# Ranking TensorE's inputs over weight conversions in the schedule of a fused attention and two-MLP kernel

## The chip, the cores and the metric

The kernel runs on one core of a Trainium2 chip. The metric is the device time of one launch in microseconds (us). Three runs of the kernel before gave 895.55, 897.68 and 898.25 us.

## The reference

An attention with random features on 4 batches, 8 heads, 576 positions and 64 channels, then two MLPs on its 2304 rows of 512 channels:

```python
q_p, k_p = phi(q * scale), phi(k * scale)      # phi: exp(x @ omega.T - sq - max) / sqrt(m), m = 128
kv = einsum('bhsm,bhsd->bhmd', k_p, v)
z = sum(k_p, axis=2)
x = einsum('bhsm,bhmd->bhsd', q_p, kv) / (einsum('bhsm,bhm->bhs', q_p, z)[..., None] + 1e-06)
x = softplus(x @ w_in) @ w_out                 # 512 -> 2048 -> 512
x = ((x @ w1) * (x @ w2)) @ w3 @ w_out2        # 512 -> 1024 -> 1024 -> 512
```

The weights of the MLPs are 64-bit floats (`view(np.int64)`), everything else is 32-bit.

## The kernel before, in words

Every product is made of three matmuls (`mm3`): each operand x is split into a rounded part hi and a rest lo = x - hi, and hi*hi, hi*lo and lo*hi are summed in PSUM. So TensorE (PE) needs two split operands for each product, and making these splits is the work of the other engines.

The program has six stages, one after the other on PE: the K features (until about 67 us), the Q features with the attention's output (until 157 us), **Up1** (the product with w_in, then softplus; until 345 us), **down1** (the product with w_out; from 348 to 610 us), **Up2** (the products with w1 and w2, multiplied; until 790 us) and **down2** (until 894 us).

- *Up1 and Up2* go by 24 "quads" each (class `Quad`): one block of weights by one block of 768 tokens, as seven products of 128x384 instead of eight. ScalarE (ACT) copies the first product to SBUF (`p6`, L479), VectorE (DVE) forms the sums u and c of products (`add`, L473), two of them on the way to further sums; ACT then applies softplus (L503) or DVE multiplies (L525), and SyncE (SP) stores the results to DRAM (gd or pd). The four PSUM banks of a quad come free when its sums have read them.
- *down1 and down2* (function `down`) go by groups of token chunks; for each of 16 (or 8) row blocks f a tile `dn` is loaded by SP four steps ahead (L569), split by ACT (`dhi`, L575) and DVE (`dlo`, L576) one step ahead (`parts(m + 1)`), and multiplied into four PSUM banks (`mult`). down1's first group holds chunks 0 and 1, and 8 banks; then come chunks 2, 3 and 4 alone. Behind the last f of a chunk its four banks are evicted to tiles `y`, even ones by DVE (L612), odd ones by ACT (L610), and SP stores them to `yd` at once (`store_y`, L723).
- *Weight conversions* (class `Job`) turn a 64-bit block into 32-bit hi and lo on the chip: a load (L119, on ACT's queue), a relu on ACT (L126), four operations on DVE (L129, L135, L142, L149), for Up1 and Up2 three sums of blocks on DVE (L156, L159, L162), the casts thi (L188) and hi (L175) on ACT, and the rests tlo (L192) and lo (L180) on GpSimd (POOL). These operations stand in a list that `step` empties at a rate beside the products. w_out, w1, w2, w3 and the last weight are converted during Up1 and down1; eight products of w3 and the last weight (`fold`) run inside down1.

Order: the framework's scheduler fixes for each engine one order of instructions, before the program runs, from the order in which they were written down and from when it takes each to be ready. Each engine then works strictly through its own list, and an instruction that waits holds up what stands behind it on that engine. The small pools matter for this: 14 buffers `M_` hold dn, dhi, dlo, y, p6 and the sums; 2 hold raw weights; 4 hold f and t of a conversion; 8 hold finished weights; PSUM has 8 banks.

Of the kernel before, what the change touches and what calls it, by code (L numbers as in the profile page):

```python
# [19 lines left out]
F32 = mybir.dt.float32  # L20
# [3 lines left out]
AF = mybir.ActivationFunctionType  # L24
ALU = mybir.AluOpType
# [30 lines left out]
FOLD_RATE = 7.0  # L56
FOLD_AT = [42 + 3 * j for j in range(8)]
KEEP = 4


@with_exitstack
def body(ctx: ExitStack, tc: tile.TileContext, q, k, k_rest, v, v_rest, om_t, w_in, w_out, w12, w3, wo, out):
    nc = tc.nc
# [9 lines left out]
    def ps():  # L73
        return ps_.tile([128, 512], F32, tag="ps", name="ps")

    def mt(n=512, dt=F32, name="m"):
        return M_.tile([128, n], dt, tag="m", name=name)
# [10 lines left out]
    def mm3(o, ahi, alo, bhi, blo, first, last, **kw):  # L88
        matmul(o, ahi, bhi, first, False, **kw)
        matmul(o, ahi, blo, False, False, **kw)  # L90
        matmul(o, alo, bhi, False, last, **kw)
# [3 lines left out]
    yd = dr.tile([128, KD, NT], F32, name="yd")  # L95
# [15 lines left out]
    class Job:  # L111
        def __init__(self, src, n, place, pool, sums=False):
            self.src, self.n, self.place, self.pool, self.sums, self.done = src, n, place, pool, sums, False
            self.slots = 4 if sums else 2
            self.kept = None

        def load(self):
            self.raw = L_.tile([128, self.n], I64, tag="l", name="raw")
            nc.scalar.dma_start(out=self.raw, in_=self.src)  # L119

        def words(self, i, dt):
            return self.raw.bitcast(dt).rearrange("p (n w) -> p n w", w=2)[:, :, i]
# [77 lines left out]
    def job_ops(jobs):  # L200
        ops = [jobs[0].load, jobs[0].relu] + [x.load for x in jobs[1:2]]
        late = []
        for i, x in enumerate(jobs):
            ops += [x.floor, x.bits_a] + late + [x.bits_b, x.bits_c]
            y = [] if x.kept else x.splits()
            late = [x.spill] if x.kept else []
            nxt = [jobs[i + 2].load] if i + 2 < len(jobs) else []
            at = next((n + 1 for n, z in enumerate(y) if isinstance(z, tuple)), len(y))
            ops += y[:at] + nxt + y[at:]
            if i + 1 < len(jobs):  # L210
                ops.append(jobs[i + 1].relu)
        return ops + late

    def reload_ops(jobs):
        ops = [x.reload for x in jobs[:1]]
        for x, y in zip(jobs, jobs[1:] + [None]):
            z = x.splits()
            ops += z[:4] + ([y.reload] if y else []) + z[4:]
        return ops
# [13 lines left out]
    def step(rate):  # L233
        due[0] += rate
        while due[0] > 0:
            if not pump_one():
                due[0] = min(due[0], 2.0)
                break
            due[0] -= 1
# [5 lines left out]
    def need(x):  # L245
        until(lambda: x.done)

    win = [Job(w_in[i], 1024, jt, "J", True) for i in range(NF // 2)]
# [159 lines left out]
    def operands(c, src, pool):  # L408
# [27 lines left out]
        a11, a21 = lambda: a[0][0], lambda: a[0][1]  # L436
        a12, a22 = lambda: a[1][0], lambda: a[1][1]
        ops = [load(0), load(1)]
        ops += parts("a11", a11)
        ops += [total("s1", a21, a22, ALU.add), total("s2", lambda: s["s1"], a11, ALU.subtract)]  # L440
# [8 lines left out]
    class Quad:  # L449
# [20 lines left out]

        def add(self, y, bank, name):
            z = mt(N, name=name)
            nc.vector.tensor_tensor(out=z, in0=bank, in1=y, op=ALU.add)  # L473
            return z

        def begin(self):
            p6 = mt(N, name="p6")
            b1 = self.product("t2", "s2")
            nc.scalar.copy(out=p6, in_=b1)  # L479
            self.b2 = self.product("t3", "s3")  # L480
            self.b3 = self.product("t1", "s1")
            self.b0 = self.product("b11", "a11")
            self.u2 = self.add(p6, self.b0, "u2")
            u3 = self.add(self.u2, self.b2, "u3")
            self.c22 = self.add(u3, self.b3, "c22")
# [10 lines left out]
    class Up1(Quad):  # L496
# [3 lines left out]

        def put(self, dst, src, f, t):
            t = self.t + t * N
            nc.scalar.activation(out=dst, in_=src, func=AF.Softplus)  # L503
            nc.sync.dma_start(out=gd[2 * self.i + f][:, t:t + N], in_=dst)

        def begin(self):
# [11 lines left out]
    class Up2(Quad):  # L518
# [3 lines left out]

        def put(self, x, y, t):
            t = self.t + t * N
            nc.vector.tensor_tensor(out=y, in0=x, in1=y, op=ALU.mult)  # L525
            nc.sync.dma_start(out=pd[self.j][:, t:t + N], in_=y)

        def finish(self):
# [31 lines left out]
    def down(src, nf, weight, store, groups, before=None, tail=1):  # L560

        seq = [(*chunks[c], f) for g in groups for f in range(nf) for c in g]
        got, split_, acc = {}, {}, {}

        def load(m):
            if m < len(seq):
                t0, n, f = seq[m]
                got[m] = mt(n, name="dn")
                nc.sync.dma_start(out=got[m], in_=src[f][:, t0:t0 + n])  # L569

        def parts(m):
            if m < len(seq):
                n = seq[m][1]
                hi, lo = mt(n, FR, "dhi"), mt(n, FR, "dlo")
                nc.scalar.copy(out=hi, in_=got[m])  # L575
                nc.vector.tensor_tensor(out=lo, in0=got.pop(m), in1=hi.bitcast(F32), op=ALU.subtract)  # L576
                split_[m] = hi, lo

        def mult(m, d):
            t0, n, f = seq[m]  # L580
            hi, lo = split_[m]
            mm3(acc[t0][d], *weight(f, d), hi, lo, f == 0, f == nf - 1)
            if f == nf - 1:
                store(d, t0, n, acc[t0][d])

        for m in range(AHEAD):
            load(m)
        parts(0)
        yield
        for m, (t0, n, f) in enumerate(seq):  # L590
            if f == 0:
                acc[t0] = [ps()[:, :n] for _ in range(KD)]
            load(m + AHEAD)
            parts(m + 1)
            if before:
                before(m, f)
            if m < len(seq) - tail:
                for d in range(KD):
                    mult(m, d)
                split_.pop(m)  # L600
            step(DOWN_RATE[m // NF] if before else 1.0)
        for d in range(KD):
            for m in range(len(seq) - tail, len(seq)):
                mult(m, d)
        yield

    def evict_down(d, src, n, name):
        o = mt(n, name=name)
        if d % 2:
            nc.scalar.copy(out=o, in_=src)  # L610
        else:
            nc.vector.tensor_copy(out=o, in_=src)  # L612
        return o


# [39 lines left out]
    ln = LQ + LN  # L655
    lx = ln + XSLACK
    xo = {}
    queue += job_ops(win[:2])
    for u in range(nq + lx + 2):
        if u >= LQ and u - LQ < nq:  # L660
# [33 lines left out]
    for s in range(NW):  # L694
        n = min(WB, NF * 512 - WB * s)
# [9 lines left out]
    wo_j.append(Job(wo[NJ - 1], 512, lambda name: spare[name == "lo"], None))  # L705
    w12_k = w12_j[KEEP:]
    w3_j = [Job(w3[j], 1024, jt, "J") for j in range(NJ)]

    def fold(j):
        need(w3_j[j])  # L710
        acc = ps()
        for i in range(NJ):
            a = 128 * i
            mm3(acc, w3_j[j].hi[:, a:a + 128], w3_j[j].lo[:, a:a + 128], wo_j[i].hi, wo_j[i].lo, i == 0, i == NJ - 1)
        o = mt(name="w34")
        nc.scalar.copy(out=o, in_=acc)
        nc.sync.dma_start(out=wd[j], in_=o)
        free["J"] += 2
        if j == NJ - 1:
            free["X1"] += 2 * (NJ - 1)  # L720

    def store_y(d, t0, n, src):
        nc.sync.dma_start(out=yd[:, d, t0:t0 + n], in_=evict_down(d, src, n, "y"))  # L723

    def before_1(m, f):
        if m in FOLD_AT:
            fold(FOLD_AT.index(m))
            step(FOLD_RATE)
        last = min(NW - 1, (4 * f + 3) // (WB // 128))
        need(wout[last])  # L730
        if m > NF * (len(DOWN) - 1) and f:
            for s in range((4 * f - 4) // (WB // 128), NW):
                if 6 * s + 5 < 4 * f and not wout[s] in given:
                    given.append(wout[s])
                    free[wout[s].pool] += 2

    given = []
    d1 = down(gd, NF, w_slot, store_y, [[0, 1], [2], [3], [4]], before_1)

    def after_1(c):  # L740
# [5 lines left out]
    ready.clear()  # L746
    for x, f in zip(w12_k, wf[KEEP:]):
        x.kept = f
    queue += job_ops(wo_j + w3_j[:4] + [x for p in zip(w12_k, w3_j[4:]) for x in p] + w12_j[:2])
    for c in range(2):  # L750
        xo[c], ops = operands(c, yd, f"X{c}")
        queue += ops
    next(d1)
    for x in wout:
        if x not in given:
            free[x.pool] += 2


    xo[2], ops = operands(2, yd, "X1")
    queue += ops + job_ops(w12_j[2:KEEP]) + reload_ops(w12_k)  # L760
    w34 = {}
# [24 lines left out]
    def store_out(d, t0, n, src):  # L786
        nc.sync.dma_start(out=out[128 * d:128 * d + 128, t0:t0 + n], in_=evict_down(d, src, n, "o"))
# [77 lines left out]
```

## Time and profile before

| what | value |
|---|---|
| three runs | 895.55, 897.68, 898.25 us (median 897.68) |
| the profiled execution | 895.84 us, of which the span of instructions is 894.1 us |
| busy in the span: PE, its weight loads, DVE, ACT, POOL | 96%, 86%, 67%, 42%, 20% |
| mean granted clock of PE | 0.989 of full speed |

Times in the trace are microseconds from the start of the span. A busy share is an average over six stages, so stretches are read apart. A name such as `dlo<-dn,dhi` is the tile written and the tiles read; in the lists of waits the waiting instruction stands to the left of `<-`, what released it to the right.

### The profile page before, as it was taken

What the parts mean: (1) busy time and instruction counts of PE and PEld (TensorE: products, weight loads), DVE (VectorE), ACT (ScalarE), POOL (GpSimd) and SP (SyncE); (2) the same over time, 40 slices, a digit from 0 to 9 for tenths busy, and PEclk for the clock granted to TensorE, in tenths of its full rate; (3) what the DMA queues carried; (4) which work ended last, traced back from release to release, by engine and by line L of the source; (5) the groups of instructions that cost most, each with busy time, mean ns of one, the idle gap of its engine ahead of it and who ended that gap; (6) DMA issues with size and microseconds to landing.
All of it is one profiled execution on the core that took longest, in us unless ns stands there. A gap on an engine that the chain in (4) does not pass through costs nothing.

```text
span 894.1 us, 14621 instructions
## 1 busy us (share of the span) xinstructions
PE 856.4 (96%) x5496; PEld 766.3 (86%) x5496; DVE 600.5 (67%) x932; ACT 379.8 (42%) x796; POOL 179.0 (20%) x110
## 2 busy tenths in 40 slices
PE   6999999999998998999889999999999999999998
PEld 5887888999998997888668887899999999988887
DVE  4795788998755578887957676258995665563322
ACT  5686889554444355444343342153411111132221
POOL 2453321022122242222221121100132222000000
PEclk9997999999999999999999999999999999999999
DMA  9511454555543447656586763154322221364432
GB/s 356 190 66 48 120 167 131 186 200 200 184 147 111 168 154 259 218 181 232 170 285 226 259 247 131 59 166 140 137 101 77 77 71 54 108 216 142 141 118 95
DMA packets 72535, 141.68 MB, mean 158 GB/s; under 512 B 7056, under 2 KB 39952, under 8 KB 69392
## 3 DMA queue, kind: packets, MB, share of 16 engines
q1 hardware_dynamic: 65696, 100.89, 33.6%
q10 hardware_dynamic: 6768, 39.85, 13.4%
q8 instruction: 43, 0.70, 0.3%
q14 instruction: 28, 0.23, 0.1%
HBM read 94.05 MB, written 46.66 MB: 157 GB/s over the span
## 4 chain that ended last, share of the span: by engine, by line
PE 65%; DVE 15%; DMA 9%; issue 5%; ACT 3%; POOL 1%; SPq 1%; ACTq 0%; DVEq 0%; POOLq 0%
PE ps L86 63%; DVE f L129 2%; DVE f L142 2%; DVE c L473 2%; DVE f L149 2%; DMA dn<-gd 2%; DMA xq<-xd 2%; PE ps L367 1%; DVE f L135 1%; DMA raw<-in_w 1%; DVE s L422 1%; DMA xq<-yd 1%; DVE dlo L576 1%; DVE u L473 1%; PE ps L397 1%
## 5 line engine op out<-in xcount | busy, mean ns | idle before, releaser
L180 POOL TENSOR_TENSOR lo<-f,hi 128x512 fp32r<-128x512 f32 (+3 forms) x58 | 95.6, 1659 | 203.0 <-ACT hi L175 158.0
L576 DVE TENSOR_TENSOR dlo<-dn,dhi 128x512 fp32r<-128x512 f32 (+1 forms) x120 | 91.3, 775 | 57.2 <-ACT dhi L575 52.6
L86 PE MATMUL ps<-dhi,hi 128*128 128x512 f32 (+1 forms) x320 | 119.2, 378 | 9.0 <-ACT dhi L575 9.0
L86 PE MATMUL ps<-dlo,hi 128*128 128x512 f32 (+1 forms) x320 | 121.0, 379 | 1.5 <-DVE dlo L576 1.4
L86 PE MATMUL ps<-dhi,lo 128*128 128x512 f32 (+1 forms) x320 | 120.3, 376 | 0.0
L192 POOL TENSOR_TENSOR tlo<-t,thi 128x1024 fp32r<-128x1024 f32 x16 | 39.1, 2443 | 292.5 <-ACT thi L188 207.8
L575 ACT CAST dhi<-dn 128x512 fp32r<-128x512 f32 (+1 forms) x120 | 67.4, 575 | 45.3 <-PE ps L86 16.3
L86 PEld LDWEIGHTS ps<-dhi,hi 128*128 128x128 f32 x320 | 60.4, 190 | 22.1 <-ACT dhi L575 10.6
L86 PEld LDWEIGHTS ps<-dlo,hi 128*128 128x128 f32 x320 | 61.1, 191 | 15.5 <-DVE dlo L576 3.6
L473 DVE TENSOR_TENSOR c<-ps,u 128x384 f32<-128x384 f32 x144 | 72.1, 550 | 0.9
L473 DVE TENSOR_TENSOR u<-ps,p 128x384 f32<-128x384 f32 x48 | 26.6, 554 | 67.6 <-PE ps L86 66.8
L129 DVE SCALAR_TENSOR_TENSOR f<-raw,f 128x1024 f32<-128x1024 f32 (+2 forms) x43 | 49.4, 1150 | 32.2 <-ACT f L126 31.8
L86 PEld LDWEIGHTS ps<-dhi,lo 128*128 128x128 f32 x320 | 60.9, 190 | 11.7
L126 ACT ACTIVATE f<-raw 128x1024 f32<-128x1024 f32 (+2 forms) x43 | 42.7, 996 | 65.8 <-DMA raw<-in_w 40.8
L175 ACT CAST hi<-f 128x1024 fp32r<-128x1024 f32 (+2 forms) x42 | 38.8, 924 | 64.7 <-DVE f L149 37.7
L503 ACT ACTIVATE c<-c 128x384 f32<-128x384 f32 x72 | 35.2, 521 | 65.3 <-DVE c L473 62.2
L479 ACT COPY p<-ps 128x384 f32<-128x384 f32 x48 | 22.8, 476 | 94.2 <-PE ps L86 89.7
L86 PE MATMUL ps<-dhi,w34l 128*128 128x512 f32 (+1 forms) x160 | 59.5, 373 | 0.0
L86 PE MATMUL ps<-dlo,w34h 128*128 128x512 f32 (+1 forms) x160 | 59.5, 373 | 0.0
L308 DVE TENSOR_REDUCE nmax<-ps 128x4 f32<-128x512 f32 x72 | 47.9, 683 | 15.6 <-PE ps L86 6.2
L86 PE MATMUL ps<-dhi,w34h 128*128 128x512 f32 (+1 forms) x160 | 57.8, 373 | 0.3 <-ACT dhi L575 0.3
L142 DVE SCALAR_TENSOR_TENSOR f<-raw,f 128x1024 int32<-128x1024 int32 (+2 forms) x43 | 52.7, 1228 | 0.7
(147 smaller groups left out, 2168.9 us busy)
## 6 DMA issues: line engine op xcount, KB each, us to landing
gd<-c SPq DMA_DIRECT2D x96, 192.0 KB, 2.2
dn<-gd SPq DMA_DIRECT2D x64, 256.0 KB, 3.6
raw<-in_w ACTq DMA_DIRECT2D x16, 1024.0 KB, 6.5
pd<-c SPq DMA_DIRECT2D x48, 192.0 KB, 1.9
raw<-in_w_in ACTq DMA_DIRECT2D x8, 1024.0 KB, 5.5
dn<-pd SPq DMA_DIRECT2D x32, 256.0 KB, 4.0
raw<-in_w_out ACTq DMA_DIRECT2D x10, 768.0 KB, 4.5
rawq<-in_q SPq DMA_DIRECT2D x18, 256.0 KB, 2.8
```

Of the source, the lines that this page charges most:

```text
L86: nc.tensor.matmul(out=o, lhsT=a, rhs=b, start=start, stop=stop, **kw)
L126: nc.scalar.activation(out=self.f, in_=self.words(1, F32), func=AF.Relu, scale=-1.0)
L129: nc.vector.scalar_tensor_tensor(out=self.f, in0=self.words(1, F32), scalar=SMALLEST, in1=self.f, op0=ALU.max, op1=ALU.max)
L142: nc.vector.scalar_tensor_tensor(out=fi, in0=self.words(1, I32), scalar=-0x40000000, in1=fi, op0=ALU.bitwise_and, op1=ALU.bitwise_or,)
L175: nc.scalar.copy(out=self.hi, in_=self.f)
L180: nc.gpsimd.tensor_tensor(out=self.lo[:, a:b], in0=self.f[:, a:b], in1=self.hi[:, a:b].bitcast(F32), op=ALU.subtract)
L192: nc.gpsimd.tensor_tensor(out=self.tlo, in0=self.t, in1=self.thi.bitcast(F32), op=ALU.subtract)
L308: nc.vector.tensor_reduce(out=nmax, in_=pj, axis=AX.X, op=ALU.max, negate=True)
L473: nc.vector.tensor_tensor(out=z, in0=bank, in1=y, op=ALU.add)
L503: nc.scalar.activation(out=dst, in_=src, func=AF.Softplus)
L575: nc.scalar.copy(out=hi, in_=got[m])
L576: nc.vector.tensor_tensor(out=lo, in0=got.pop(m), in1=hi.bitcast(F32), op=ALU.subtract)
```

## The change

1. Six kinds of instruction are emitted under `tc.high_priority(300)`, which ranks them in the scheduler as if they had been written down 300 instructions earlier: the sums of quads, the copy p6, softplus, the multiplication, the evictions y and o, and the splits dhi and dlo. No operation is added and none taken away.
2. In `down`, the splits are made two steps ahead (`parts(m + 2)`, and `parts(0)`, `parts(1)` before the first).
3. In down1, the stores of y are issued a step later: they wait in a list `late`, which is emptied at the next step whose f is not 0, and once behind the last step.
4. The loads of the first two blocks of w_in go to SP's queue in place of ACT's.

```diff
--- before.py
+++ after.py
@@ -56,6 +56,7 @@
 FOLD_RATE = 7.0
 FOLD_AT = [42 + 3 * j for j in range(8)]
 KEEP = 4
+URGENT = 300
 
 
 @with_exitstack
@@ -112,11 +113,11 @@
         def __init__(self, src, n, place, pool, sums=False):
             self.src, self.n, self.place, self.pool, self.sums, self.done = src, n, place, pool, sums, False
             self.slots = 4 if sums else 2
-            self.kept = None
+            self.kept = self.queue = None
 
         def load(self):
             self.raw = L_.tile([128, self.n], I64, tag="l", name="raw")
-            nc.scalar.dma_start(out=self.raw, in_=self.src)
+            (self.queue or nc.scalar).dma_start(out=self.raw, in_=self.src)
 
         def words(self, i, dt):
             return self.raw.bitcast(dt).rearrange("p (n w) -> p n w", w=2)[:, :, i]
@@ -470,13 +471,15 @@
 
         def add(self, y, bank, name):
             z = mt(N, name=name)
-            nc.vector.tensor_tensor(out=z, in0=bank, in1=y, op=ALU.add)
+            with tc.high_priority(URGENT):
+                nc.vector.tensor_tensor(out=z, in0=bank, in1=y, op=ALU.add)
             return z
 
         def begin(self):
             p6 = mt(N, name="p6")
             b1 = self.product("t2", "s2")
-            nc.scalar.copy(out=p6, in_=b1)
+            with tc.high_priority(URGENT):
+                nc.scalar.copy(out=p6, in_=b1)
             self.b2 = self.product("t3", "s3")
             self.b3 = self.product("t1", "s1")
             self.b0 = self.product("b11", "a11")
@@ -500,7 +503,8 @@
 
         def put(self, dst, src, f, t):
             t = self.t + t * N
-            nc.scalar.activation(out=dst, in_=src, func=AF.Softplus)
+            with tc.high_priority(URGENT):
+                nc.scalar.activation(out=dst, in_=src, func=AF.Softplus)
             nc.sync.dma_start(out=gd[2 * self.i + f][:, t:t + N], in_=dst)
 
         def begin(self):
@@ -522,7 +526,8 @@
 
         def put(self, x, y, t):
             t = self.t + t * N
-            nc.vector.tensor_tensor(out=y, in0=x, in1=y, op=ALU.mult)
+            with tc.high_priority(URGENT):
+                nc.vector.tensor_tensor(out=y, in0=x, in1=y, op=ALU.mult)
             nc.sync.dma_start(out=pd[self.j][:, t:t + N], in_=y)
 
         def finish(self):
@@ -572,8 +577,9 @@
             if m < len(seq):
                 n = seq[m][1]
                 hi, lo = mt(n, FR, "dhi"), mt(n, FR, "dlo")
-                nc.scalar.copy(out=hi, in_=got[m])
-                nc.vector.tensor_tensor(out=lo, in0=got.pop(m), in1=hi.bitcast(F32), op=ALU.subtract)
+                with tc.high_priority(URGENT):
+                    nc.scalar.copy(out=hi, in_=got[m])
+                    nc.vector.tensor_tensor(out=lo, in0=got.pop(m), in1=hi.bitcast(F32), op=ALU.subtract)
                 split_[m] = hi, lo
 
         def mult(m, d):
@@ -586,12 +592,13 @@
         for m in range(AHEAD):
             load(m)
         parts(0)
+        parts(1)
         yield
         for m, (t0, n, f) in enumerate(seq):
             if f == 0:
                 acc[t0] = [ps()[:, :n] for _ in range(KD)]
             load(m + AHEAD)
-            parts(m + 1)
+            parts(m + 2)
             if before:
                 before(m, f)
             if m < len(seq) - tail:
@@ -606,10 +613,11 @@
 
     def evict_down(d, src, n, name):
         o = mt(n, name=name)
-        if d % 2:
-            nc.scalar.copy(out=o, in_=src)
-        else:
-            nc.vector.tensor_copy(out=o, in_=src)
+        with tc.high_priority(URGENT):
+            if d % 2:
+                nc.scalar.copy(out=o, in_=src)
+            else:
+                nc.vector.tensor_copy(out=o, in_=src)
         return o
 
 
@@ -655,6 +663,8 @@
     ln = LQ + LN
     lx = ln + XSLACK
     xo = {}
+    for x in win[:2]:
+        x.queue = nc.sync
     queue += job_ops(win[:2])
     for u in range(nq + lx + 2):
         if u >= LQ and u - LQ < nq:
@@ -720,9 +730,15 @@
             free["X1"] += 2 * (NJ - 1)
 
     def store_y(d, t0, n, src):
-        nc.sync.dma_start(out=yd[:, d, t0:t0 + n], in_=evict_down(d, src, n, "y"))
+        y = evict_down(d, src, n, "y")
+        late.append(lambda: nc.sync.dma_start(out=yd[:, d, t0:t0 + n], in_=y))
+
+    late = []
 
     def before_1(m, f):
+        if f:
+            while late:
+                late.pop(0)()
         if m in FOLD_AT:
             fold(FOLD_AT.index(m))
             step(FOLD_RATE)
@@ -751,6 +767,8 @@
         xo[c], ops = operands(c, yd, f"X{c}")
         queue += ops
     next(d1)
+    while late:
+        late.pop(0)()
     for x in wout:
         if x not in given:
             free[x.pool] += 2
```

Line numbers of the changed kernel are higher by 1 to 18 than those of the kernel before. Three places show how the orders differ.

VectorE in Up1 at quad 16 (at 285 us in the trace), the kernel before, then the changed one. L129 to L149 (L130 to L150) are a conversion of w_out; u and c are the sums of the quad, u first:

```order
L129 SCALAR_TENSOR_TENSOR f<-raw,f 128x768
L473 TENSOR_TENSOR u_3806<-ps,p_3764 128x384
L135 TENSOR_SCALAR f<-f 128x768
L473 TENSOR_TENSOR u_3808<-ps,u_3806 128x384
L142 SCALAR_TENSOR_TENSOR f<-raw,f 128x768
L473 TENSOR_TENSOR c_3810<-ps,u_3808 128x384
L473 TENSOR_TENSOR c_3821<-ps,u_3727 128x384
L473 TENSOR_TENSOR c_3832<-ps,u_3727 128x384
L149 SCALAR_TENSOR_TENSOR f<-raw,f 128x768
```

```order
L475 TENSOR_TENSOR u_3806<-ps,p_3764 128x384
L130 SCALAR_TENSOR_TENSOR f<-raw,f 128x768
L475 TENSOR_TENSOR u_3808<-ps,u_3806 128x384
L136 TENSOR_SCALAR f<-f 128x768
L475 TENSOR_TENSOR c_3810<-ps,u_3808 128x384
L475 TENSOR_TENSOR c_3821<-ps,u_3727 128x384
L475 TENSOR_TENSOR c_3832<-ps,u_3727 128x384
L143 SCALAR_TENSOR_TENSOR f<-raw,f 128x768
L150 SCALAR_TENSOR_TENSOR f<-raw,f 128x768
```

The first u now stands ahead of L130 (L129 before) and the third operation of the conversion behind the sums; L130 and L136 still stand among them.

VectorE in down1 where the first group ends (438 to 450 us), before, then changed. y are evictions, dlo are splits for coming steps:

```order
L129 SCALAR_TENSOR_TENSOR f<-raw,f 128x1024 x2
L135 TENSOR_SCALAR f<-f 128x1024 x2
L142 SCALAR_TENSOR_TENSOR f<-raw,f 128x1024 x2
L149 SCALAR_TENSOR_TENSOR f<-raw,f 128x1024
L612 COPY y<-ps 128x512 x2
L149 SCALAR_TENSOR_TENSOR f<-raw,f 128x1024
L576 TENSOR_TENSOR dlo<-dn,dhi 128x512
L612 COPY y<-ps 128x512 x2
```

```order
L130 SCALAR_TENSOR_TENSOR f<-raw,f 128x1024
L136 TENSOR_SCALAR f<-f 128x1024
L620 COPY y<-ps 128x512
L143 SCALAR_TENSOR_TENSOR f<-raw,f 128x1024
L620 COPY y<-ps 128x512
L150 SCALAR_TENSOR_TENSOR f<-raw,f 128x1024
L582 TENSOR_TENSOR dlo<-dn,dhi 128x512
L620 COPY y<-ps 128x512 x2
```

Before, seven operations of two conversions stand between the last split and the first eviction; now two do, and the other evictions stand one or two apart.

ScalarE at the step from Up1 to down1 (350 to 357 us), before, then changed. c are the softplus operations of Up1's last quads, hi the cast of a conversion of w_out:

```order
L503 ACTIVATE c_4314<-c_4314 128x384
L575 CAST dhi<-dn 128x512
L175 CAST hi<-f 128x768
L119 DMA raw<-in_w_out 128x768
L503 ACTIVATE c_4337<-c_4337 128x384
L503 ACTIVATE c_4348<-c_4348 128x384
L503 ACTIVATE c_4359<-ps 128x384
```

```order
L507 ACTIVATE c_4314<-c_4314 128x384
L581 CAST dhi<-dn 128x512
L176 CAST hi<-f 128x768
L581 CAST dhi<-dn 128x512
L120 DMA raw<-in_w_out 128x768
L507 ACTIVATE c_4341<-c_4341 128x384
L507 ACTIVATE c_4352<-c_4352 128x384
L507 ACTIVATE c_4363<-ps 128x384
```

The split of down1's second step now stands ahead of the last three softplus operations instead of behind them; that of the third step follows them.

## Rows read from the trace of the kernel before

**Rows 1.** The page's first part: busy time of the engines over the whole span.
```profile
PE 856.4 (96%) x5496; PEld 766.3 (86%) x5496; DVE 600.5 (67%) x932; ACT 379.8 (42%) x796; POOL 179.0 (20%) x110
```

**Rows 2.** PE's waits, whole span: waiting line, releaser: total us, times, longest.
```profile
PE ps L86 <- DVE c L473: 9.6, 7, 3.2
PE ps L86 <- ACT dhi L575: 9.3, 4, 4.4
PE ps L86 <- DMA rawk<-in_k: 7.0, 1, 7.0
PE ps L367 <- ACT qp L313: 2.5, 2, 2.1
PE ps L86 <- DVE u L473: 1.9, 4, 0.9
...
PE ps L86 <- DVE dlo L576: 1.4, 4, 0.6
PE ps L86 <- ACT kpr L313: 1.0, 1, 1.0
```

**Rows 3.** Windows: stretch, us; busy us of PE, PEld, DVE, ACT, POOL; clock; DMA.
```profile
69.50:79.70 10.20, 10.20 (x94) 8.04 (x93) 2.83 (x4) 4.54 (x14) 3.98 (x4) 0.50 0.10 28
315.26:318.67 3.41, 3.41 (x12) 3.41 (x12) 0.99 (x2) 2.79 (x6) 2.67 (x2) 0.50 0.68 186
356.22:359.63 3.41, 3.41 (x10) 2.65 (x9) 1.02 (x2) 0.64 (x1) 0.00 (x0) 0.50 1.02 367
448.38:451.79 3.41, 3.41 (x10) 2.63 (x9) 1.56 (x3) 1.82 (x3) 3.41 (x2) 0.50 0.94 322
```

**Rows 4.** DMA issues, first 30 us: times, KB each, median us to landing.
```profile
raw<-in_w_in ACTq DMA_DIRECT2D x2, 1024.0 KB, 6.8
...
rawk<-in_k SPq DMA_DIRECT2D x4, 128.0 KB, 5.2
```

**Rows 5.** Timeline of ACT, K to Q: start, us, instruction, [idle before it].
```profile
67.99 1.04 ACT L188 CAST thi<-t 128x1024 fp32r<-128x1024 f32 x1 [1.08 <-DVE t L162]
```

**Rows 6.** Timeline of DVE in Up1, quad 16.
```profile
285.19 0.96 DVE L129 SCALAR_TENSOR_TENSOR f<-raw,f 128x768 f32<-128x768 f32 x1 [2.10 <-ACT f L126]
286.07 0.55 DVE L473 TENSOR_TENSOR u<-ps,p 128x384 f32<-128x384 f32 x1
286.53 0.55 DVE L135 TENSOR_SCALAR f<-f 128x768 int32<-128x768 int32 x1
...
287.47 0.95 DVE L142 SCALAR_TENSOR_TENSOR f<-raw,f 128x768 int32<-128x768 int32 x1
288.33 1.48 DVE L473 TENSOR_TENSOR c<-ps,u 128x384 f32<-128x384 f32 x3
```

**Rows 7.** Timeline of ACT in Up1, ahead of the same place.
```profile
279.78 1.05 ACT L175 CAST hi<-f 128x1024 fp32r<-128x1024 f32 x1
280.72 0.48 ACT L479 COPY p<-ps 128x384 f32<-128x384 f32 x1
```

**Rows 8.** PE's waits from 346 to 360 us, Up1 to down1.
```profile
PE ps L86 <- ACT dhi L575: 3.5, 1, 3.5
```

**Rows 9.** Timeline of ACT from 350 to 357 us.
```profile
353.77 0.60 ACT L575 CAST dhi<-dn 128x512 fp32r<-128x512 f32 x1
...
355.08 0.61 ACT L575 CAST dhi<-dn 128x512 fp32r<-128x512 f32 x1
```

**Rows 10.** Timeline of DVE from 437 to 455 us, end of down1's first group.
```profile
438.30 1.21 DVE L129 SCALAR_TENSOR_TENSOR f<-raw,f 128x1024 f32<-128x1024 f32 x1
...
445.73 1.28 DVE L612 COPY y<-ps 128x512 f32<-128x512 f32 x2
```

**Rows 11.** Timeline of SP's queue from 440 to 455 us.
```profile
440.43 7.87 SPq L723 DMA_DIRECT2D yd<-y  x4
448.40 1.40 SPq L569 DMA_DIRECT2D dn<-gd  x2
```

**Rows 12.** PE's waits from 610 to 790 us, Up2.
```profile
PE ps L86 <- DVE c L473: 0.9, 1, 0.9
PE ps L86 <- DVE u L473: 0.9, 1, 0.9
```

**Rows 13.** Tile dlo from 357 to 446 us, first group: count, ns min/median/max.
```profile
L576 DVE TENSOR_TENSOR dlo<-dn,dhi x29: 679/687/2881, 360.4 to 437.7; 128x512 fp32r<-128x512 f32 x29
```

**Rows 14.** Windows, down1's first group; columns as in rows 3.
```profile
357.00:446.00 89.00, 86.52 (x366) 69.25 (x364) 74.56 (x88) 36.92 (x58) 21.63 (x13) 0.99 0.60 202
```

## The prediction

> **What bounds the kernel now.** First the busy shares of the page: PE is busy 856.4 of the 894.1 us of the span, VectorE 67%, ScalarE 42% [rows 1]. PE bounds the kernel, and the change takes no matmul away. So it can only save time in which PE stands still, or in which it runs at the lower of its two clocks. Second, then, PE's list of waits [rows 2]: leaving out small ones, 9.6 + 9.3 + 2.5 + 1.9 + 1.4 + 1.0 = 25.7 us go on sums (c, u), splits (dhi, dlo) and the features qp and kpr, none on weights, and 7.0 us on the first load. Third, the windows with a granted clock below 1: four stretches, 10.2 + 3 x 3.41 = 20.4 us, at 0.50, that is 1.2 instead of 2.4 GHz [rows 3]. Work done there would take half as long at full clock, so they cost 10.2 us. Each begins shortly behind one of the long waits. All that ranking can win is thus 25.7 + 10.2 = 35.9 us, and a little of the first load. The timelines tell how much of each piece the new order really reaches.
>
> **The change, place by place.** A wait that is a matter of order shrinks by what no longer stands ahead of its releaser; a slow stretch goes if the gap ahead of it goes, which no row can promise.
>
> *Start.* PE waits 7.0 us for the K loads [rows 2]. The two 1 MB loads of w_in share the DMA engines with them: a K piece takes 5.2 us from issue to landing [rows 4]. On SP they stand among later loads. Bounds: nothing, if the time is latency, and about half of 5.2 us, if the K pieces then get twice the share. omega and its split come first on the same path, so I take **-1.2**.
>
> *K features.* The 1.0 us on kpr [rows 2] is a conversion on VectorE ahead of a maximum. In the new order conversions spread between maxima: **-1.0**; bounds 0 and 1.0.
>
> *K to Q.* The longest wait for qp is 2.1 us [rows 2]. ScalarE stood 1.08 us idle at the cast thi, which waited for the last sum of the conversion on VectorE (L162), and qp stood behind thi [rows 5]. The 10.2 us at half clock follow [rows 3]. In the new order that conversion is finished earlier and qp ranks ahead. Bounds: 0, and 2.1 + 5.1 = 7.2. Both halves hang on one short chain which the order plainly changes, so I take **-6.0**. What is moved there has a price: the second conversion, seven operations on VectorE and three casts on ScalarE, now runs inside the Q features. Those engines stand a third idle or more over the whole span [rows 1], so 0 is one end; the other is one wait like the longest for qp, twice: +4.2. I take **+1.5**.
>
> *Up1.* Of the sums' 9.6 us, 0.9 lie in Up2 [rows 12], 8.7 here. At quad 16 VectorE did L129 at 285.19 (it had waited for the relu on ScalarE), then u, L135, u, L142 and three c, the last ending at 288.33 + 1.48 [rows 6]. In the new order L142 follows the sums (288.33 - 287.47 = 0.86 saved) and the first u precedes L129 (286.53 - 286.07 = 0.46 saved). But the cast hi now stands behind the copy p, so hi, POOL's lo, the relu and L129 all come later by p's own 0.48, less a little overlap: 0.47 [rows 7]. Net 0.85 of the 3.2 us. The order has the same pattern at quad 19: another 0.85. At a third quad it is the same before and after: nothing. Half of the slow stretch at 315, 1.7 us, may go with its gap: I count half, 0.85. The shorter waits: 1.0. Together **-3.5**; bounds 0 and 8.7 + 1.0 + 1.7.
>
> *Up1 to down1.* PE waits 3.5 us for a dhi [rows 8], the one that ScalarE does at 353.77, behind softplus and a conversion's cast; the next follows at 355.08 [rows 9]. Now the former stands ahead of the last three softplus operations, but the next still follows them. I leave 0.9 of 3.5 + 1.7 (the stretch at 356): **-4.3**; bounds 0 and 5.2.
>
> *End of down1's first group.* The longest wait of all for a split, 4.4 us [rows 2]. From 438.30 to 445.73 VectorE works on two conversions; the first eviction y comes after that [rows 10], and until it no PSUM bank is free. On SP the stores of y, issued 440.43, hold the queue until the loads dn start at 448.40 [rows 11]; a second wait of about 1.1 us (the rest of 9.3 - 4.4 - 3.5 is 1.4 in two waits) follows from that, and half of the stretch at 448 is 1.7. In the new order two operations stand ahead of the first eviction, 1.21 us and less each, loads alternate with stores, and splits are a step ahead. I take **-7.0** of 7.2; bounds 0 and 7.2. If the cover goes (14 buffers hold 8 y and three pairs of splits at once), loads of dn come late, and the 1.1 us stays.
>
> *Elsewhere in down1* dlo waits 1.4 us in all [rows 2]; two steps ahead: **-1.0**. Of this a rule of the Trainium skill says something. First the rows: in the first group dlo takes 679 ns at least, 687 in the median and 2881 at most [rows 13], one instruction in one shape, and POOL is busy there for a quarter of the time [rows 14]. The Trainium skill (SBUF — State Buffer, section "SBUF: two separate sides") says that a VectorE operation with two inputs in SBUF and a GpSimd operation exclude each other: whichever starts first holds a shared pair of ports until its end. The spread of dlo agrees. By the page, rank cannot shorten this wait, since POOL is in possession. The row's worth of that: 2881 - 687 = 2.2 us; if both large dhi/dlo places of down1 meet it, 4.4 us of the gains stay away and the time is some 877.
>
> *Up2.* u and c wait 0.9 + 0.9 [rows 12] behind a conversion's L135; in the new order sums stand together, about -1.8. But one conversion's cast thi moves a quad later, and its rest is then late by an estimated 0.8. **-1.0**; bounds -1.8 and +1.
>
> *down2* and the tail keep their order: 0. Softplus and multiplications off PE's path cost nothing, as SP's stores of gd and pd do not bind.
>
> **Sum:** 1.2 + 1.0 + 6.0 - 1.5 + 3.5 + 4.3 + 7.0 + 1.0 + 1.0 = 23.5 us. The profiled execution took 895.84, 1.84 below the median of the runs; 895.84 - 23.5 = 872.3. I say **872**.
>
> **The rivals.**
>
> *A. Order helps only where a split or feature is late.* The waits for dhi (4.4 + 3.5), qp (2.1) and kpr (1.0) go, 11.0 us; the sums still stand behind L129, the clock falls all the same, and the late conversions cost 1.5 + 1.0. Gain 8.5: **887**. For it: the order at quad 16 shows two conversion operations still among the sums. Against: three slow stretches follow gaps that shrink most.
>
> *B. Everything goes,* 25.7 + 10.2 + 2 at the start: **858**. For it: each long wait has an operation in its way that now ranks below. Against: three places where the order is the same.
>
> *C. Splits clog VectorE (slower).* In the first group VectorE is busy 74.56 of 89.00 us, 14.4 to spare [rows 14]. The splits, two steps ahead and first in rank, start whether or not PE needs them; those that run into POOL's lo last up to 2.2 us longer [rows 13]. If all 29 did, 64 us would be added; conversions of w_out would fall behind and PE wait for weights. It decides when 14.4 + 23.5 = 37.9 us are added, 1.3 us for each. At 1.6 us each: 46 - 14.4 = 32 us lost, **904**. Against: the median dlo is undisturbed, and POOL's work does not grow. The trace has no wait for weights.
>
> *D. The orders differ but the time does not:* each stall is only handed on to the next late conversion, since the operations are the same. **895**. Against: VectorE has slack in all stages.
>
> **How the numbers follow.** This case 57%, with its own range 864 to 880; A 20%; B 12%; C 7%; D 4%. The range of 8 in 10 takes this case, most of B's side and A's: **859 to 887**. About 0.3% (2.7 us) is what a measurement of this kernel can tell from no change. Faster by more than that: this case, A and B, 0.89 less a little for the unlisted: 0.88; same 0.05; slower 0.07.
>
> **What would show it.** In the new list of waits of PE, dhi and qp fall from 11.8 to under 2 us, c from 9.6 to about 6 with one wait over 2 us left at quads 16 and 19. The windows show full clock behind K to Q and at 450 us. The first y of chunk 0 ends within 3 us of its last matmul. The first matmul starts near 5.8 us. Wrong would be: waits for hi, lo or tlo of weights (C), half clock still for 20 us (A), stalls of equal sum at new places (D).

## The result, and the profile after

The changed kernel took 882.37 us in the median of four runs (880.43 to 883.07), the kernel before, beside it, 896.62 us (893.27 to 898.25). The ratio is 0.9842, 95% interval 0.9808 to 0.9877. The forecast was 872 with a range of 859 to 887: faster, as forecast, and inside the range, but with 14.3 us gained where 23.5 were expected.

The profiled execution has a span of 881.0 us, 13.1 less than before. First the page's busy line, then PE's list of waits, which answers to [rows 2], and the windows at half clock, which answer to [rows 3], all of the changed kernel:

```profile
PE 850.9 (97%) x5496; PEld 763.9 (87%) x5496; DVE 597.6 (68%) x932; ACT 381.8 (43%) x796; POOL 177.9 (20%) x110
```

```profile
PE ps L87 <- DVE c L475: 8.5, 5, 2.3
PE ps L87 <- DVE dlo L582: 4.8, 3, 4.3
PE ps L87 <- DMA rawk<-in_k: 4.0, 1, 4.0
PE ps L398 <- DVE xt L389: 4.0, 4, 1.7
PE ps L87 <- DVE xt L389: 1.4, 1, 1.4
PE ps L87 <- ACT xs1h L430: 1.4, 1, 1.4
PE ps L87 <- POOL tlo L193: 1.0, 2, 0.8
PE ps L87 <- DVE xs3l L433: 0.6, 1, 0.6
PE ps L87 <- ACT xs3h L430: 0.4, 1, 0.4
PE ps L368 <- ACT qp L314: 0.4, 1, 0.4
PE ps L87 <- ACT dhi L581: 0.3, 1, 0.3
```

```profile
231.54:234.95 3.41, 3.41 (x13) 3.41 (x12) 2.56 (x5) 1.29 (x2) 0.00 (x0) 0.50 0.97 312
443.17:450.00 6.83, 5.05 (x12) 3.99 (x13) 5.22 (x6) 3.78 (x5) 2.37 (x1) 0.50 0.96 354
```

The waits for dhi (9.3 us), qp (2.5), kpr (1.0) and u (1.9) are gone or small, and so are the 10.2 us at half clock where Q begins. In their place stand waits that the list of before lacked or had short: dlo 4.8 (4.3 of it in one), xt 5.4 in all (a single 1.5 before), xs1 and xs3 2.4. Of the slow stretches two are left within the work, 3.41 and 6.83 us long, where four were.

By place, in us of PE's time, from the two traces: waits, and half of PE's busy time in each slow stretch (2.5 of 5.05 in the longer one), which stands behind a plus sign where the two are given apart:

| place | before | after | gain | forecast |
|---|---|---|---|---|
| first load | 7.0 | 4.0 | 3.0 | 1.2 |
| K features (kpr) | 1.0 | 0 | 1.0 | 1.0 |
| K to Q (qp, clock) | 7.2 | 0 | 7.2 | 6.0 |
| Q features (xt) | 1.5 | 5.4 | -3.9 | -1.5 |
| Up1 (c, u, xs; clock) | 9.7 + 1.7 | 10.3 + 1.7 | -0.6 | 3.5 |
| Up1 to down1 (c, dhi, dlo, clock) | 3.7 + 1.7 | 1.2 | 4.2 | 4.3 |
| end of down1's first group | 5.5 + 1.7 | 4.3 + 2.5 | 0.4 | 7.0 |
| rest of down1 | 1.1 | 0.3 | 0.8 | 1.0 |
| Up2 (c, u; then tlo) | 1.8 | 0.8 | 1.0 | 1.0 |

The gains add up to 13.1 us, as the spans have it. Three rows fail: the end of the first group, Up1, and Q.

**The end of the first group.** VectorE and ScalarE of the changed kernel at the place that answers to [rows 10]: start, us, instruction, [idle before it].

```profile
436.25 0.69 DVE L582 TENSOR_TENSOR dlo<-dn,dhi 128x512 fp32r<-128x512 f32 x1
436.85 1.28 DVE L620 COPY y<-ps 128x512 f32<-128x512 f32 x2
438.05 2.99 DVE L130 SCALAR_TENSOR_TENSOR f<-raw,f 128x1024 f32<-128x1024 f32 x1
441.08 0.69 DVE L136 TENSOR_SCALAR f<-f 128x1024 int32<-128x1024 int32 x1
441.81 1.23 DVE L143 SCALAR_TENSOR_TENSOR f<-raw,f 128x1024 int32<-128x1024 int32 x1
443.07 1.23 DVE L150 SCALAR_TENSOR_TENSOR f<-raw,f 128x1024 int32<-128x1024 int32 x1
444.21 1.28 DVE L582 TENSOR_TENSOR dlo<-dn,dhi 128x512 fp32r<-128x512 f32 x2
```

```profile
438.28 1.14 ACT L581 CAST dhi<-dn 128x512 fp32r<-128x512 f32 x2
```

VectorE's evictions end at 438.13 and PE waits for no bank; that part came true. But two splits dhi are ready by 439.42, and their dlo start at 444.21, because all four operations of a conversion stand between the evictions and the splits on VectorE. PE waits 4.3 us for them, until 444.95, and runs at half clock from 443.17 to 450.00.

**Up1.** ScalarE at 174 us, then VectorE at 226 and POOL beside it:

```profile
173.79 0.48 ACT L482 COPY p<-ps 128x384 f32<-128x384 f32 x1 [1.29 <-PE ps L87]
174.17 0.84 ACT L430 CAST xs3h<-s 128x768 fp32r<-128x768 f32 x1
176.68 1.13 ACT L127 ACTIVATE f<-raw 128x1024 f32<-128x1024 f32 x1 [1.68 <-DMA raw<-in_w_in]
177.71 0.82 ACT L430 CAST xs1h<-s 128x768 fp32r<-128x768 f32 x1
```

```profile
226.13 2.96 DVE L150 SCALAR_TENSOR_TENSOR f<-raw,f 128x1024 int32<-128x1024 int32 x1
229.01 1.48 DVE L475 TENSOR_TENSOR c<-ps,u 128x384 f32<-128x384 f32 x3
```

```profile
224.58 3.43 POOL L193 TENSOR_TENSOR tlo<-t,thi 128x1024 fp32r<-128x1024 f32 x1 [11.62 <-ACT thi L189]
```

In the first, two casts of token operands, which have no rank, stand behind other work: xs3h behind the ranked copy p, which waits 1.29 us for PE's product, and xs1h behind a relu that waits for its load. In the second a conversion's last operation, 2.96 us long beside POOL's work where its kind takes 1.2, stands ahead of three ranked sums; PE waits 2.3 us for them, and the stretch of 3.41 us at half clock follows.

**Q.** Before, PE's waits for xt were one line:

```profile
PE ps L397 <- DVE xt L388: 1.5, 1, 1.5
```

Now they are five waits. The longest but one lies behind this piece of VectorE's work at 113 us: a sum of the token operands waits for its load, and xt, which PE waits 1.4 us for, stands behind it.

```profile
112.89 0.96 DVE L423 TENSOR_TENSOR s<-xq 128x768 f32<-128x768 f32 x1 [2.53 <-DMA xq<-xd]
...
114.70 0.42 DVE L389 TENSOR_TENSOR xt<-ps,den 128x256 f32<-128x256 f32 x1
```

### The profile page after: what moved, and what is told of

Read it like the earlier page. It is cut to its first block, busy times and chain, and to the rows that moved or that the text cites. A ratio compares the mean times of both kernels' runs of the same rounds, so it can differ in the third digit from the quotient of the medians.

```text
span 881.0 us, 14617 instructions
## 1 busy us (share of the span) xinstructions
PE 850.9 (97%) x5496; PEld 763.9 (87%) x5496; DVE 597.6 (68%) x932; ACT 381.8 (43%) x796; POOL 177.9 (20%) x110
## 4 chain that ended last, share of the span: by engine, by line
PE 53%; DVE 4%; DMA 2%; issue 1%; ACT 1%; POOL 0%; ACTq 0%; DVEq 0%; POOLq 0%
PE ps L87 53%; DMA raw<-in_w 1%; DVE f L150 1%; DMA dn<-gd 1%; DVE f L143 1%; DVE dlo L582 0%; DVE f L130 0%; DMA raw<-in_wo 0%; DVE f L136 0%; ACT dhi L581 0%; DVE c L475 0%; DVE u L475 0%; ACT hi L176 0%; POOL tlo L193 0%; ACT f L127 0%
## 5 line engine op out<-in xcount | busy, mean ns | idle before, releaser
L181 POOL TENSOR_TENSOR lo<-f,hi 128x512 fp32r<-128x512 f32 (+3 forms) x58 | 93.2, 1621 | 195.1 <-ACT hi L176 162.5
L582 DVE TENSOR_TENSOR dlo<-dn,dhi 128x512 fp32r<-128x512 f32 (+1 forms) x120 | 89.0, 752 | 62.6 <-ACT dhi L581 44.1
L87 PEld LDWEIGHTS ps<-dlo,hi 128*128 128x128 f32 x320 | 60.8, 190 | 17.7 <-DVE dlo L582 6.2
L130 DVE SCALAR_TENSOR_TENSOR f<-raw,f 128x1024 f32<-128x1024 f32 (+2 forms) x43 | 51.0, 1188 | 33.2 <-ACT f L127 33.0
L150 DVE SCALAR_TENSOR_TENSOR f<-raw,f 128x1024 int32<-128x1024 int32 (+2 forms) x43 | 53.1, 1236 | 0.6
```

The source lines that it names most:

```text
L87: nc.tensor.matmul(out=o, lhsT=a, rhs=b, start=start, stop=stop, **kw)
L130: nc.vector.scalar_tensor_tensor(out=self.f, in0=self.words(1, F32), scalar=SMALLEST, in1=self.f, op0=ALU.max, op1=ALU.max)
L150: nc.vector.scalar_tensor_tensor(out=fi, in0=self.words(0, I32), scalar=29, in1=fi, op0=ALU.logical_shift_right, op1=ALU.bitwise_or,)
L181: nc.gpsimd.tensor_tensor(out=self.lo[:, a:b], in0=self.f[:, a:b], in1=self.hi[:, a:b].bitcast(F32), op=ALU.subtract)
```

## The experiments

The four parts of the change can be undone one by one. Theory 1, formed on the trace after: the moved loads made the difference in the K and Q stages, two steps ahead that at the start of down1, and the ranks act on the sums alone. The rival: ranks carry the gain, as the change's size suggests. All ratios are to the kernel before, run beside.

**e1: all but the moved loads.**

```diff
-    for x in win[:2]:
-        x.queue = nc.sync
```

> The changed kernel with the first two loads of w_in back on ACT's queue. Theory 1 (the moved loads, not the ranks, changed the K and Q stages and the first quads): PE's first wait returns from 4.0 to 7.0 us, a wait for qp of about 2 us with half clock behind it returns where Q begins (7 us), the waits for xt near 115 to 130 us and the ones for xs3, xs1 near 175 to 179 us go (some 7 us): 884 to 889 us. Rival (the ranks ordered the Q stage): no long wait for qp returns, about 883 to 886, by the start alone.

888.31 us, ratio 0.9906 (0.9892 to 0.9921). PE's waits of this kernel, and the window where Q begins:

```profile
PE ps L87 <- DMA rawk<-in_k: 6.9, 1, 6.9
...
PE ps L368 <- ACT qp L314: 2.9, 2, 2.1
PE ps L398 <- DVE xt L389: 1.6, 2, 1.5
PE ps L87 <- ACT xs1h L430: 1.4, 1, 1.4
...
PE ps L87 <- ACT kpr L314: 1.0, 1, 1.0
```

```profile
70.86:81.10 10.24, 10.24 (x103) 8.28 (x104) 2.58 (x3) 4.54 (x13) 4.39 (x4) 0.50 0.10 28
```

The first wait, kpr, qp and the 10 us at half clock are all back, and xt is short again. So all of the K and Q rows of the table, good and bad, belong to two loads that moved. The waits for xs1 and xs3 stayed (1.4 and 0.9 us): theory 1 had put them with the loads, wrongly.

**e2: the moved loads alone** (ranks, second step ahead and late stores taken out of the changed kernel).

> The kernel before with only the first two loads of w_in moved to SP's queue. Theory 1: first wait about 4 us, no wait for kpr and for qp of over 1 us, but new waits in the Q stage and the first quads; the rest as before: 889 to 894 us. Rival (the ranks ordered the Q stage): only the start is shorter, 893 to 894, with the 2.1 us wait for qp and the 10 us at half clock still there.

890.66 us, 0.9930 (0.9906 to 0.9953). The first wait is 4.0 us, kpr and the long qp are gone, PE waits 5.0 us for xt and 9.1 for dhi, and not at all for xs1 or xs3. That is the mirror image of e1. The last two are in e1 and not here, so they come with something that e1 kept and e2 took out; e3 and e6 show that it is the ranks.

**e3: the ranks alone.**

> The kernel before with only the ranks (sums, copy, softplus, product, evictions, splits). Theory 1 (ranks act on the sums of quads alone): the waits for c shrink by 3 to 5 us in Up1 and Up2, dhi still waits 3.5 us where down1 begins and 4.4 us where its first group ends: 890 to 894 us. Rival (ranks carry the gain): 883 to 886, with dhi's waits under 2 us.

894.08 us, 0.9972 (0.9955 to 0.9989). Its longest waits:

```profile
PE ps L87 <- ACT dhi L581: 8.8, 3, 4.2
PE ps L87 <- DVE c L475: 7.7, 4, 2.3
PE ps L87 <- DMA rawk<-in_k: 7.1, 1, 7.1
```

The part of the change that the title names is worth 2.5 us alone, of 896 (1.0 to 4.0 by the interval). c falls only from 9.6 to 7.7, xs1 and xs3 come in, and the two long waits for dhi stay (3.5 and 4.2 us) though dhi has the rank. The rival is out.

**e4: all but the second step ahead.**

```diff
-        parts(1)
...
-            parts(m + 2)
+            parts(m + 1)
```

> The changed kernel with the splits one step ahead again. Theory 1 (two steps ahead is what took the 3.5 us of dhi at the start of down1, and at the end of the first group it only put dlo's wait of 4.3 us in place of dhi's 4.4): dhi waits 3.5 us and 4.4 us again, dlo's 4.3 us goes: 886 to 889 us. Rival (ranks of dhi and dlo did both): no change, 881 to 884.

889.33 us, 0.9919 (0.9904 to 0.9934), a little above what was expected.

```profile
PE ps L87 <- ACT dhi L581: 9.2, 4, 3.5
```

dhi is back at 9.2 us, the 4.3 of dlo are gone. In this kernel's order seven conversion operations stand ahead of the first eviction again, as before. So the new order at the end of the first group, conversion ahead of dlo included, comes from splitting two steps ahead. Not all of the 7 us need be down1's: this trace has three slow stretches ahead of down1, at 116, 178 and 263 us, where that of the change has one, at 231. What they have to do with the edit is not shown.

Theory 2 then says of that place: the wait is the conversion that stands ahead of the splits, and an order without it saves 7 to 8 us. Rival: buffers or stores are late there in any order.

**e5: dn loaded five steps ahead** (`AHEAD = 5`), which puts the splits between the conversion's operations at that place.

> The changed kernel with dn loaded five steps ahead in place of four. In the order this puts the splits dlo between the operations of the conversions where down1's first group ends, in place of a whole conversion ahead of them. Theory 2 (the 4.3 us of dlo and the 6.8 us at half clock behind it come from that conversion standing ahead of the splits): both go, 7 to 8 us: 874 to 877 us. Rival (something there has to be late, buffers or stores): another wait of 3 us or more takes its place, 880 to 884.

879.69 us, 0.9814 (0.9774 to 0.9854); span 877.8. Its window at the end of the first group, and PE's waits there (436 to 452 us):

```profile
440.00:450.00 10.00, 8.94 (x38) 6.70 (x37) 10.00 (x13) 4.51 (x7) 1.26 (x1) 1.00 0.88 292
```

```profile
PE ps L87 <- ACT dhi L581: 0.7, 1, 0.7
PE ps L87 <- DVE dlo L582: 0.4, 1, 0.4
```

4.3 us of waits became 1.1 and the clock stays at its upper level, worth 2.5: 5.7 us saved at the place, with most of what theory 2 had expected. But the loads ahead changed the start of down1 too, where PE now waits 3.0 us (1.6 for dlo, 0.7 for dhi, 0.7 for c) instead of 1.2, with a new stretch of 3.41 us at half clock: 3.5 us lost. That leaves 2.2 of the 3.2 us by which the spans differ; the medians differ by 2.7, so the time expected was missed by 3 to 6 us. In this order L130 does not run beside POOL's work as it does in the change, where that costs it 1.8 us (the section on the prediction has the rows), so a part of the gain can come from there and not from the place of the splits.

**e6: all but the ranks.**

> The changed kernel without any rank (splits two steps ahead, late stores and moved loads stay). Theory 2 (ranks are worth about 2 us, their gain on c and u being taken back by xs3, xs1 and a new wait for c): 883 to 886 us, with c near 9.9 us, no wait for xs1 or xs3, and dlo's 4.3 us unchanged. Rival (ranks carry the gain together with the splits): 889 to 893.

886.25 us, 0.9886 (0.9836 to 0.9936), just above the theory's range, with c at 10.7 us, no wait for xs1 or xs3, and dlo's 4.1 us unchanged. Without the ranks the median is 3.9 us higher, while the interval of this ratio alone is 4.5 us to either side: the ranks seem to be worth something in the changed kernel too, and not the main part.

**e7: y stored at once.**

> The changed kernel with y stored at once, not a step late. Theory 2 (the stores are of no matter, the order of splits and conversions on VectorE is the same): 881 to 884 us, dlo's wait still 3 to 4.5 us. Rival (late stores free SP's queue for loads): 886 to 890, with a wait for dhi on a late load of dn.

886.06 us, 0.9883 (0.9845 to 0.9921): not the no change that theory 2 had expected. dhi and dlo wait 1.9 us near the end of down1's last groups (0.3 with late stores), so the late stores do free something there; this is 1.6 of 3.7 us. The rest would be half-clock stretches at 117, 178 and 287 us, before any y is stored, where the change has one. What the edit has to do with them was not found.

**e8: the token operands ranked too**, their sums, casts and rests under the same `tc.high_priority`.

> The changed kernel with Up1's and Up2's token operands (their sums, casts and rests) ranked too. Theory 2 (the new waits for xs3 and xs1 come from a relu of a conversion, which waits for its 1 MB load, standing ahead of casts that are not ranked): these 2.4 us go, 879 to 881 us. Rival (they come from the late load itself): no change, 882 to 883.

882.16 us, 0.9829 (0.9776 to 0.9882). The waits for xs1 and xs3 are gone, as expected, but the time is not the 879 to 881 expected: c has risen from 8.5 to 11.0 us, and new waits stand elsewhere (2.0 us for a dhi at 356 us, 2.1 in all for qp).

```profile
PE ps L87 <- DVE c L478: 11.0, 8, 2.3
```

At 211 us PE now waits 2.3 us for sums; three operations of a conversion stand ahead of them or among them there, one in the changed kernel. That the ranked casts moved the conversion there is the likely reason, but not shown.

**e9: five steps ahead only from step 21 on,** so that the start of down1 keeps its order.

```diff
-            load(m + AHEAD)
+            load(m + AHEAD + (1 if m > 20 else 0))
+            if m == 20:
+                load(m + AHEAD + 1)
```

> The changed kernel with dn five steps ahead from step 21 of down1 and down2 on, so that the start of down1 keeps its order; at the end of the first group one split dlo now stands ahead of the whole conversion, the next ones still behind it. Theory 2 (dlo's 4.3 us is the conversion ahead of it): one step's 12 matmuls, 2.8 us, now cover that much, dlo's wait falls to 1 to 2 us and the 6.8 us at half clock to 3.4 or nothing; no new wait at the start of down1: 876 to 879 us. Rival (loads and stores are what is late there): the wait stays above 3 us, 881 to 883.

881.27 us, 0.9806 (0.9773 to 0.9840), above the 876 to 879 expected. At the end of the first group PE waits for three things, and ScalarE's dhi shows why:

```profile
PE ps L87 <- ACT dhi L581: 2.0, 1, 2.0
PE ps L87 <- DVE dlo L582: 1.5, 1, 1.5
PE ps L87 <- ACT y L620: 0.6, 1, 0.6
```

```profile
442.64 0.62 ACT L581 CAST dhi<-dn 128x512 fp32r<-128x512 f32 x1 [3.67 <-DMA yd<-y]
```

dlo's wait fell to 1.5 us, as theory 2 worked out, but dhi now waits for a store of y to give up its buffer: the rival is right as well. In this order the buffers, 14 of them, look like the next limit; no run had more. In e5 dhi waits for stores of y at this place too, 2.2 us on ScalarE, but PE loses only 0.7 by it.

**e10: e9, with den and xt of the attention ranked.**

> As e9, and the attention's denominators and products xt ranked too. Theory 2 (Q's waits for xt come from operations of the token operands and of the moved conversions ahead of xt on VectorE, which are of no rank): the 5.4 us of waits for xt fall by 1.5 to 3 us, 874 to 877. Rival (VectorE and ScalarE are full there, so that any order loses the same): other waits of the Q stage take their place, as e9.

878.94 us, 0.9775 (0.9737 to 0.9813). PE's waits in the Q stage, 60 to 157 us, where e9 had 4.8 us for xt:

```profile
PE ps L399 <- DVE xt L390: 1.4, 1, 1.4
PE ps L368 <- ACT qp L314: 1.0, 1, 1.0
```

2.4 us less, and the medians differ by 2.3, though the time is above the 874 to 877 expected. The loss in Q was order too, not full engines. The median of this version is the lowest of those tried, 3.4 us below that of the change (6 by the ratios to the kernels run beside); the 0.8 us to e5 are not settled.

## Why the prediction was right, and where not

**Right.** PE's waits and slow stretches were what could be won, and of their 35.9 us 10.1 were, net, besides 3.0 at the start. Up1 to down1 gave 4.2 us for 4.3 forecast, and e4 shows the cause: split two steps ahead, dhi's 3.5 us go, and without it they return. In Up2 the sums' 1.8 us went and the late tlo of 0.8 us came, for a net 1.0. At quad 16 the wait fell from 3.2 to 1.9, 1.3 us for 0.85. The slower rival C did not show: the median dlo is 685 ns, and no wait for w_out's weights appears. Rival D, given 4%, did in part: in the three rows that fail, stalls were handed on to new places (dlo 4.3, xt 3.9, the sums' 2.3 at 230 us, xs 2.4).

**The step that failed most: "In the new order two operations stand ahead of the first eviction ... I take -7.0".** The count ahead of the evictions was right. What stands behind them, a whole conversion ahead of the next splits, follows directly on the quoted rows of the order, and was not weighed. Its price could be had: four operations of about 1.2 us at most, as in [rows 10], under 5 us. Nor was it only the banks that waited in the kernel before, as the prediction had it. ScalarE had evicted one y at 439.85, and the split dhi for which PE waited stood behind a cast of the same conversion:

```profile
445.85 1.04 ACT L175 CAST hi<-f 128x1024 fp32r<-128x1024 f32 x1 [5.44 <-DVE f L149]
447.27 0.62 ACT L575 CAST dhi<-dn 128x512 fp32r<-128x512 f32 x1
```

So the splits had to be freed of the conversion, not the evictions alone. Measured in the changed kernel were 6.2 us, from 438.05 to 444.21, of which 4.3 became PE's wait. So dlo took the place of dhi, and the gain was 0.4. e5 shows that 5.7 us more were to be had there.

The conversion took longer than its operations do alone. L130 started at 438.05, while POOL was at work on this:

```profile
437.55 2.41 POOL L181 TENSOR_TENSOR lo<-f,hi 128x1024 fp32r<-128x1024 f32 x1 [7.09 <-ACT hi L176]
```

POOL's operation ended at 439.96, and L130 at 441.04, 1.1 us later: it took 2.99 us where it takes 1.21 otherwise. The copies of y out of PSUM, which ran as POOL started, took their usual time. By the Trainium skill (SBUF — State Buffer, "SBUF: two separate sides"), a VectorE operation with two inputs in SBUF and a GpSimd operation that reads SBUF exclude each other, and one with at most one input in SBUF, outside its two-port modes, is free of that. The trace agrees, with 1.8 us. The prediction had allowed for it on dlo itself; it hit the conversion ahead of dlo.

**Up1: "Together -3.5".** The place lost 0.6 us instead, and c came to 8.5 us where the signs named about 6. The named quads gave what was said. Not seen were the casts xs, which were not ranked and so fell behind a ranked copy (xs3, 1.0 us) and a relu with a late load (xs1, 1.4), and a conversion that moved ahead of the sums of another quad (2.3 us and a slow stretch of 3.41). Ranking some of the things that PE waits for pushes back the ones left out.

**K to Q: right size, wrong owner.** "In the new order that conversion is finished earlier and qp ranks ahead": qp has no rank in the diff. The order there changed since the two loads moved, and with them when the conversions can begin: e1 and e2 show it from both sides. On SP the first of the two is issued at 35 us, where ACT's queue had both at the start, and the relu of the second conversion comes at 69.69 instead of 54.67, behind the step from K to Q. That the size fits is luck.

```profile
35.01 0.43 SPq L120 DMA_DIRECT2D raw<-in_w_in  x1
```

**Q: -3.9 for -1.5**, near the bound of 4.2: the second conversion and the sums of the token operands, some with late inputs, stand ahead of xt. The prediction took VectorE's and ScalarE's idle share over the whole span for room here; and the wait for xt, 1.5 us in the list of before, was not among those that it counted. **Start: 3.0 for 1.2**: without the 2 MB beside them the first K pieces land 2.7 us after issue instead of 5.2 [rows 4], and omega 2.1 instead of 4.5, so nearly all of it was the company of the two loads.

```profile
rawk<-in_k SPq DMA_DIRECT2D x4, 128.0 KB, 2.7
```

By parts, the change less each: loads 5.7 us (0.9906 - 0.9842), second step ahead 6.9, ranks 3.9, late stores 3.7. They add to 20.2, more than the 14.2 of the whole: if that is more than noise, some of the gain needs two parts at once. The last two are about as large as their intervals.

## What to carry to other kernels

Where a schedule is changed, read the new order both ahead of what is urgent and behind it, up to the next instruction that the bounding engine needs: an operation that is pushed back lands somewhere. A rank alone need not move an instruction: in e3 dhi had it, and both its long waits stayed. A likely reason, not shown here, is that a rank chooses only among instructions that the scheduler takes to be ready. And undo each part of a change alone before naming the one that worked: here two moved loads brought more than the ranks (0.9930 alone against 0.9972).

## What was not expected

The same program differs between executions with its granted clock. The four runs of e8 took 884.93, 883.52, 880.80 and 876.20 us at mean clocks of 0.990, 0.992, 0.994 and 0.998. At 0.990, two hundredths of the span are at half clock, 17.7 us that cost 8.8; at 0.998 they cost 1.8. That is 7.0 of the 8.7 us between them. Between kernels it looks the same: PE waits 1.3 to 1.7 us for xt at 114 to 115 us in the traces of the change, e4, e5, e7, e8 and e9, and a slow stretch follows in those of e4, e7 and e9 alone. So a stall's second cost, the slow stretch behind it, comes in some executions and not in others, and differences of 2 us between single kernels here, e5 against e9 for one, are not settled by four runs.
